# Output row built on eight neighbouring partitions of 128 columns with zero-padded weights, stored as eight rows, with filler matmuls between the last weight pieces

## Chip, cores, metric

One core of a Trainium2 chip. The metric is device time in microseconds (us); I quote the median of several executions. Times inside a profile are counted from the start of its span, which is shorter than the measured time (381.1 against 382.4 for the kernel before).

Names in the profile: PE is the matmul engine and PEld its weight loads; DVE is the vector engine, which makes the cast; POOL fills buffers at the start; SPq is the sequencer that issues the loads and the store; SBUF is the on-chip memory. The granted clock is the share of the full matmul clock that PE was allowed: below, warm is 1.00 and cold is 0.50.

## Reference

One decode token: an attention block over a cache of 65,536 keys with 4 key/value heads and 32 query heads, mixed by a scalar gate with a small gated MLP. What matters here is the end of it.

```python
q = (x @ wq)                                  # 1 x 4096, 32 heads of 128
o = softmax(q k^T * Dh**-0.5) v               # k, v: 4 heads x 65536 x 128, bf16
a = o.reshape(1, 1, 4096) @ wo                # wo: 4096 x 1024   <- the tail of the kernel
b = gmlp(x)                                   # 1 x 1024
return g * a + (1 - g) * b                    # 1 x 1024, bf16
```

The inputs are 162 MB, read once.

## The kernel before

One long stream of loads (keys, values and weights) runs on one queue through a ring of buffers. The `wo` matrix is the last 8 MB: pieces 0, 1 and 2 of 2 MB, then piece 3 in cuts of 5, 2 and 1 row blocks. A row block is 128 rows of `wo` by 1024 columns. A store of zeros stands ahead of the last load in the queue; the real store comes at the end.

```python
# constants:  QW = DO // 4   (256 columns), ovec: one column of 128 per row block, 32 of them
osrc = bass.AP(tensor=arena, offset=OFF["OROW"], ap=[[32 * NA, 4], [1, QW]])   # rows 0, 32, 64, 96

def store():
    P("SP", lambda e: e.dma_start(out[0, 0].rearrange("(q n) -> q n", n=QW), osrc), ...)

# ... the gated MLP's share (four partial rows) is summed into fb first, by float32 matmuls with
# start=True ("e4" picks the partitions 0, 32, 64, 96), long before the tail ...

out_first(3)            # softmax denominators of the last head
out_rest(3)             # normalise, select, fill ovec for the last 8 row blocks

for i, c0, c1 in [(0, 0, 8), (1, 0, 8), (2, 0, 8)] + [(3, c0, c1) for c0, c1 in WO_CUT]:
    sl, keys = use(("wo", i, c0))
    def f(e, i=i, sl=sl, c0=c0, c1=c1):
        for c in range(c0, c1):
            for q in range(4):                                  # four column groups of the array
                o = DO * (c - c0) + QW * q
                ins = e.matmul(fb[32*q:32*q+1, 0:QW], ovec[:, 8*i+c:8*i+c+1], sl[:, o:o+QW],
                               start=False, stop=(i == 3 and c == 7), tile_position=(0, 32*q), ...)
        return ins
    P("PE", f, r=[("ovec", i)] + keys, w=["fb"])
    # ... (the buffer is given back to the ring)
P("DVE", lambda e: e.tensor_copy(orow[0:97, :], fb[0:97, 0:QW]), w=["orow", "fb"])   # the cast
store()
```

Of the kernel before, what the change touches and what calls it, by code (L numbers as in the profile page):

```python
# [9 lines left out]
ALU = mybir.AluOpType  # L10
AXX = mybir.AxisListType.X
# [120 lines left out]
def bass_gated_mix__gqa_block_cached__mixer_gmlp__decode_kernel(  # L132
# [14 lines left out]
    G, Sk, Dh = A_k_cache.shape[1:]  # L147
# [4 lines left out]
    DO = A_wo.shape[1]  # L152
# [3 lines left out]
    FC = FH // 128  # L156
    OC = HQ * Dh // 128
# [3 lines left out]
    total = G * NP  # L161
# [3 lines left out]
    QP = 152  # L165
    NKT = 2
    NSC = 4
    QW = DO // 4
    FB4 = FH // 4
    SCALE = 1.0 / math.sqrt(Dh)  # L170
    GELU_C = 0.044715
# [4 lines left out]
    OFF = {}  # L176
    cur = 0

    def region(name, nbf):
        nonlocal cur  # L180
        OFF[name] = cur
        cur += (nbf + 15) // 16 * 16

    for name, n in [
        ("RING", NSUB * SUB), ("KT", NKT * 4096), ("SC", NSC * 2048), ("PSB", 2 * 1024), ("PTSB", 2 * 1024),
        ("QPAD", 4 * QP), ("IDB", 128), ("BM", 256), ("SEL", 16 * 32),
        ("M16", 32), ("MQ", 32), ("XT", KC), ("WB", 2), ("WBB", 4), ("ONEB", 128),
        ("MAXC", 2 * total), ("LP", 2 * total), ("COLS", 2 * 64), ("DM", 64), ("ONES", 256), ("QALL", 128), ("OV", OC), ("MHALF", 4),
        ("YB", FC), ("OROW", QW),
    ]:  # L190
        region(name, n)
    NA = (cur + 63) // 64 * 64
    arena = nc.alloc_sbuf_tensor("arena", [128, NA], BF16)

    def ab(name, n, o=0):
        return arena[:, OFF[name] + o:OFF[name] + o + n]

    def af(name, n, o=0):
        return arena[:, OFF[name] + 2 * o:OFF[name] + 2 * (o + n)].bitcast(F32)

    def vw(base, off, dims, p0=0, np_=128):
        ps = base.ap[0][0]
        return bass.AP(tensor=base.tensor, offset=base.offset + off + p0 * ps,
                       ap=[[ps, np_]] + [list(d) for d in dims])

    idb, bm, ones = ab("IDB", 128), af("BM", 128), af("ONES", 128)
# [2 lines left out]
    qpad, qall = ab("QPAD", 4 * QP), ab("QALL", 128)  # L209
    maxc, lp, colt = af("MAXC", total), af("LP", total), af("COLS", 64)  # L210
    mhalf = af("MHALF", 2)
    yb, ovec, orow = ab("YB", FC), ab("OV", OC), ab("OROW", QW)
    dm = af("DM", 32)
    psb, psb2 = ab("PSB", 1024), ab("PSB", 2048)
    osc, ot = ab("PSB", 512), af("PSB", 128, 256)
    col = lambda i: colt[:, i:i + 1]
    (C_GS, C_GE, C_G1, C_G, C_OMG, C_MU, C_V, C_S0, C_R0, C_S1, C_R1, C_AL, C_BE, C_T) = range(14)
    C_E4, C_G4 = 14, 16

    def gcol(g, i):  # L220
        return col(C_G4 + 12 * g + i)
# [11 lines left out]
    scp = nc.alloc_psum_tensor("scp", [128, 2048], F32)  # L233
# [4 lines left out]
    ob, mb, fb = obt[:, :], mbt[:, :], fbt[:, :]  # L238
    tb = scp[:, 1024:1536]
    tbh = tb.bitcast(BF16)  # L240
    KSC = lambda n: ("scp", n % 2)
# [3 lines left out]
    P = R.op  # L245
# [12 lines left out]
    m32 = af("SC", 32, 136)  # L258
# [4 lines left out]
    P("POOL", lambda e: e.tensor_copy(idb, idf), r=["idf"], w=["idb"])  # L263
    P("POOL", lambda e: e.memset(qpad, 0.0), w=["qpad"])
    P("POOL", lambda e: e.memset(orow, 0.0), w=["orow"])
    P("POOL", lambda e: e.memset(ones, 1.0), w=["ones"])
    P("POOL", lambda e: e.memset(oneb, 1.0), w=["oneb"])
    P("DVE", lambda e: e.memset(mb, 0.0), w=["mb"])
# [76 lines left out]
    WO_CUT = [(0, 5), (5, 7), (7, 8)]  # L345
# [2 lines left out]
    for c0, c1 in WO_CUT:  # L348
        load([("wo", 3, c0)], rows(A_wo, 3, 8)[:, DO * c0:DO * c1], WO_AT[3] + DO * c0)

    osrc = bass.AP(tensor=arena, offset=OFF["OROW"], ap=[[32 * NA, 4], [1, QW]])

    def store():
        P("SP", lambda e: e.dma_start(out[0, 0].rearrange("(q n) -> q n", n=QW), osrc), r=["orow"],
          w=["out"], dma="out")
# [5 lines left out]
    def grains(off, w):  # L361
        return list(range(off // GRAN, (off + w + GRAN - 1) // GRAN))

    def issue():

        while issued[0] < len(stream):
            n = issued[0]
            keys, off, src = stream[n]
            w = src.shape[1]
            gr = grains(off, w)  # L370
            if any(k not in used for x in gr if x in owner for k in owner[x]):
                return
            for j, x in enumerate(gr):
                owner[x] = (keys[j * len(keys) // len(gr)],)
            if n == len(stream) - 1:
                store()
            P("SP", lambda e, o=OFF["RING"] + off, w=w, src=src: e.dma_start(arena[:, o:o + w], src),  # L377
              w=[("slot", x) for x in gr], dma="s%d" % gr[0])
            issued[0] += 1

    def use(key):
        n, off, w = place[key]
        assert n < issued[0], key
        return arena[:, OFF["RING"] + off:OFF["RING"] + off + w], [("slot", x) for x in grains(off, w)]

    def done(key):
        used.add(key)
        issue()
# [7 lines left out]
    P("POOL", lambda e: e.tensor_copy(vw(bm, 0, [[8, 16], [1, 8]]), vw(m8, 0, [[0, 16], [1, 8]])), r=["m8"], w=["bm"])  # L396

    P("DVE", lambda e: e.tensor_reduce(m32, vw(idf, 0, [[1, 32], [32, 4]]), AXX, ALU.add), r=["idf"], w=["m32"])
    P("POOL", lambda e: e.tensor_copy(col(C_E4), m32[:, 0:1]), r=["m32"], w=["e4"])
    P("POOL", lambda e: e.tensor_copy(vw(sel, 0, [[16, 32], [1, 16]]), vw(m32, 0, [[1, 32], [0, 16]])),  # L400
      r=["m32"], w=["sel"])
    P("DVE", lambda e: e.tensor_reduce(mq, vw(idf, 0, [[1, 16], [16, 8]]), AXX, ALU.add), r=["idf"], w=["mq"])
    P("DVE", lambda e: e.tensor_reduce(mhalf, vw(idf, 0, [[32, 2], [64, 2], [1, 32]]), mybir.AxisListType.XY, ALU.add),
      r=["idf"], w=["mhalf"])
# [4 lines left out]
    for fe in range(4):  # L409
        P("POOL", lambda e, fe=fe: e.tensor_copy(vw(sele, 128 * fe, [[32, 4], [1, 32]]),  # L410
                                                vw(idb, 64 * (fe // 2) + fe % 2, [[0, 4], [2, 32]])),
          r=["idb"], w=[KSE])
# [5 lines left out]
    def f(e):  # L418
        for c in range(KC):
            ins = e.matmul(tb[:, c:c + 1], vw(xm, c, [[8, 128]], 0, 8), oneb[0:8, 0:1], start=(c == 0),  # L420
                           stop=(c == KC - 1), skip_group_check=True)
        return ins
# [3 lines left out]
      r=["oneb", "wsp", "bsp"], w=["mb"])  # L426
# [6 lines left out]
      r=["ones", "gs"], w=[KTB])  # L433
# [4 lines left out]
      r=["g"], w=["omg"])  # L438
# [3 lines left out]
    wqs, keys = use(("wq", 0))  # L442
# [105 lines left out]
    def out_first(g):  # L548
        def f(e):
            for h in range(2):  # L550
                ins = e.matmul(mb[:, 0:1], bm, lp[:, 2 * g + h:2 * g + h + 1], start=(h == 0), stop=(h == 1))  # L551
            return ins
        P("PE", f, r=["bm", ("lp", 2 * g), ("lp", 2 * g + 1)], w=["mb"])
# [19 lines left out]
    def out_fourth(g):  # L573
        P("DVE", lambda e: e.tensor_tensor(vw(ot, 0, [[8, 16], [1, 8]]), vw(mb, 0, [[8, 16], [1, 8]]),
                                           vw(mq, 0, [[1, 16], [0, 8]]), ALU.mult), r=["mq"], w=["psb", "mb"])

        def red(e):
            with nc.allow_low_precision(reason="one term is not zero"):
                return e.tensor_reduce(ovec[:, 8 * g:8 * (g + 1)], vw(ot, 0, [[1, 8], [8, 16]]), AXX, ALU.add)
        P("DVE", red, r=["psb"], w=[("ovec", g)])  # L580


# [24 lines left out]
    def mixer_rest(zw, zc, KZR, KZT):  # L607
# [27 lines left out]
        P("DVE", lambda e: e.scalar_tensor_tensor(yb, z2[:, 0:FC], col(C_OMG), h1, op0=ALU.mult, op1=ALU.mult),  # L635
          r=["z2", "omg", "zg"], w=["yb", KZR])

    def wout_piece():
        sl, keys = use(("wout", 0))

        def f(e):
            for c in range(FC):
                j = c % 4
                for s in range(2):
                    o = DO * c + 512 * s
                    ins = mm(e, s > 0, ob[32 * j:32 * j + 1, 512 * s:512 * (s + 1)], yb[:, c:c + 1], sl[:, o:o + 512],
                             start=(c < 4), stop=(c >= FC - 4), tile_position=(0, 32 * j), skip_group_check=True)
            return ins
        P("PE", f, r=["yb"] + keys, w=["ob"])
        done(("wout", 0))  # L650
        part = ab("KT", 2048, 4096).bitcast(F32)
        P("ACT", lambda e: e.activation(part[0:97, :], ob[0:97, :], ACTF.Copy), w=[("kt", 1), "ob"])

        def f(e):
            for q in range(4):
                ins = e.matmul(fb[32 * q:32 * q + 1, 0:QW], col(C_E4)[0:97, :], part[0:97, QW * q:QW * (q + 1)],
                               start=True, stop=False, tile_position=(0, 32 * q), skip_group_check=True)
            return ins
        P("PE", f, r=["e4", ("kt", 1)], w=["fb"])


    def k_step(n):

        for p in range(4):
            k_piece(n, p)
# [5 lines left out]
    def out_rest(g):  # L671
        out_second(g)
        out_third(g)
        out_fourth(g)
# [28 lines left out]
    for n in (12, 13, 14, 15):  # L703
        pv_piece(n)
        if n < 14:
            pt_half(n + 2)
    out_first(3)
    out_rest(3)


    for i, c0, c1 in [(0, 0, 8), (1, 0, 8), (2, 0, 8)] + [(3, c0, c1) for c0, c1 in WO_CUT]:
        sl, keys = use(("wo", i, c0))

        def f(e, i=i, sl=sl, c0=c0, c1=c1):
            for c in range(c0, c1):
                for q in range(4):
                    o = DO * (c - c0) + QW * q
                    ins = e.matmul(fb[32 * q:32 * q + 1, 0:QW], ovec[:, 8 * i + c:8 * i + c + 1],  # L718
                                   sl[:, o:o + QW], start=False, stop=(i == 3 and c == 7),
                                   tile_position=(0, 32 * q), skip_group_check=True)  # L720
            return ins
        P("PE", f, r=[("ovec", i)] + keys, w=["fb"])
        done(("wo", i, c0))
    P("DVE", lambda e: e.tensor_copy(orow[0:97, :], fb[0:97, 0:QW]), w=["orow", "fb"])  # L724
    store()

    R.ahead = 2
# [29 lines left out]
```

## Time and profile before

| | kernel before |
|---|---|
| time | 382.43 us (three executions, 382.40 to 382.46) |
| span of the profile | 381.1 us |
| bytes read | 162.01 MB, 425 GB/s over the span |
| PE instructions in the profile | 2176 (1383 matmuls, 793 weight loads) |

The chain that ended last, kernel before, from 370 us on: start, duration, what. One reads it as: the `wo` loads (345.52 + 31.08) are waited for until 376.60, then PE works through the cuts, then the cast.

```profile
345.52 31.08 DMA arena<-in_A_wo_dram
...
376.74 1.73 PE fbt L718 x28
...
378.50 0.41 PE fbt L718 x4
...
379.00 0.42 DVE arena L724
```

The same tail in the timeline: start, duration, engine, line, operation, count, and in brackets how long the engine sat idle and what ended it. The first weight load of each cut starts when that cut has landed, so the rows at 377.87 and 378.50 date the last two landings.

```profile
373.55 1.36 PE L718 MATMUL fbt<-arena 128*1 128x256 bf16 x32 [2.22 <-DMA arena<-in_A_wo_dram]
...
376.74 2.14 PE L718 MATMUL fbt<-arena 128*1 128x256 bf16 x32 [1.83 <-DMA arena<-in_A_wo_dram]
377.87 0.10 PEld L718 LDWEIGHTS fbt<-arena 128*1 128x1 bf16 x8 [0.40 <-DMA arena<-in_A_wo_dram]
378.50 0.09 PEld L718 LDWEIGHTS fbt<-arena 128*1 128x1 bf16 x4 [0.52 <-DMA arena<-in_A_wo_dram]
379.00 0.42 DVE L724 CAST arena<-fbt 97x256 bf16<-97x256 f32 x1 [9.98 <-PE fbt L718]
379.45 0.54 SPq L354 DMA_DIRECT2D out_dram<-arena  x1
```

The windows view of the kernel before: after the stretch come PE, weight loads, DVE, ACT and POOL (busy us and instructions), then the granted clock, the DMA share and GB/s. The clock is low during the last pieces.

```profile
373.50:376.70 3.20, 1.36 (x32) 0.72 (x32) 0.00 (x0) 0.00 (x0) 0.00 (x0) 0.60 0.89 363
376.70:378.90 2.20, 2.12 (x32) 0.73 (x32) 0.00 (x0) 0.00 (x0) 0.00 (x0) 0.50 0.22 87
```

The queue's own waits, kernel before: the store takes 1.1 us more after its issue.

```profile
SPq L121 <- DMA out_dram<-arena: 1.1, 1, 1.1
```

### The profile page before, as it was taken

The page shows a single profiled execution, that of the slowest core. Times are in us where ns is not written, and L with a number is a line of the kernel's source. Part 1 is how long each engine was busy: PE and PEld are TensorE (multiplying, and loading weights), DVE is VectorE, ACT ScalarE, POOL GpSimd, SP SyncE. Part 2 cuts the span into 40 slices and gives each one's busy share as a digit, 9 for nine tenths or more (in the row PEclk, how much of TensorE's full clock was granted, in tenths as well). Part 3 has the DMA queues.
Part 4 walks back from the last instruction along what each step waited for, and adds up shares of the span by engine and source line. Part 5 has one row for each costly group of instructions (what it writes and reads, how often), then busy time and mean ns, then how long its engine had stood idle before and what let it go on. Part 6 is the DMA issues. An engine that isn't in the chain of part 4 may idle for free.

```text
span 381.1 us, 2468 instructions
## 1 busy us (share of the span) xinstructions
PE 229.2 (60%) x1383; PEld 55.5 (15%) x793; DVE 204.5 (54%) x162; ACT 22.2 (6%) x23; POOL 7.5 (2%) x35
## 2 busy tenths in 40 slices
PE   0050487566558924893887238952995984549373
PEld 0010011111111200121111001220121111212031
DVE  3111596778489525956882249745875871402020
ACT  1000000010420000002000000022000000220000
POOL 4000000000000000000000000000000000000000
PEclk9997599698959975999798858985998896959776
DMA  9999999999999999999999999999999999999995
GB/s 440 434 433 413 426 387 437 440 492 420 428 433 392 426 442 440 433 420 433 454 428 440 440 440 440 421 433 440 392 420 439 457 433 426 426 408 433 423 430 223
DMA packets 4237, 162.15 MB, mean 426 GB/s; under 512 B 508, under 2 KB 516, under 8 KB 772
## 3 DMA queue, kind: packets, MB, share of 16 engines
q1 hardware_dynamic: 4192, 162.01, 98.7%
q8 instruction: 8, 0.13, 0.1%
q10 hardware_dynamic: 36, 0.00, 0.0%
q14 instruction: 1, 0.01, 0.0%
HBM read 162.01 MB, written 0.00 MB: 425 GB/s over the span
## 4 chain that ended last, share of the span: by engine, by line
DMA 63%; DVE 18%; PE 17%; issue 1%; ACTq 0%; SPq 0%; DVEq 0%
DMA arena<-in_A_k_cache_dram 41%; DVE arena L490 15%; DMA arena<-in_A_v_cache_dram 10%; DMA arena<-in_A_wo_dram 8%; PE scp L250 5%; DMA arena<-in_B_b_sp_dram 5%; PE scp L252 5%; PE obt L250 3%; PE obt L252 3%; DVE arena L527 1%; PE fbt L718 1%; ACTq L276 0%; DVE arena L563 0%; DVE arena L561 0%; SPq L377 0%
## 5 line engine op out<-in xcount | busy, mean ns | idle before, releaser
L490 DVE STREAM_TRANSPOSE arena<-arena 128x2048 f32<-128x2048 f32 x64 | 142.8, 2283 | 45.9 <-DMA arena<-in_A_k_cache_dram 31.3
L250 PE MATMUL scp<-arena 128*128 128x512 bf16 x256 | 108.9, 425 | 84.9 <-DVE arena L490 84.9
L252 PE MATMUL scp<-arena 128*128 128x512 bf16 x256 | 107.7, 421 | 0.0
L250 PE MATMUL obt<-arena 128*64 128x512 bf16 (+2 forms) x334 | 62.8, 416 | 21.3 <-DMA arena<-in_A_v_cache_dram 21.3
L252 PE MATMUL obt<-arena 128*64 128x512 bf16 (+2 forms) x334 | 61.9, 410 | 0.0
L250 PEld LDWEIGHTS scp<-arena 128*128 128x128 bf16 x256 | 26.9, 105 | 194.4 <-issue 99.5
L527 DVE STREAM_TRANSPOSE arena<-arena 128x2048 bf16<-128x2048 bf16 x7 | 16.2, 2311 | 31.3 <-PE obt L252 29.1
L250 PEld LDWEIGHTS obt<-arena 128*64 128x64 bf16 (+1 forms) x334 | 18.3, 113 | 74.5 <-issue 56.9
L522 ACT ACTIVATE arena<-arena 128x2048 bf16<-128x2048 f32 x8 | 16.0, 2003 | 218.1 <-DVE arena L519 195.0
L507 DVE TENSOR_SCALAR_CACHE_REDUCE arena<-scp 128x2048 f32<-128x2048 f32 x8 | 18.3, 2292 | 16.0 <-PE scp L252 16.0
L568 PE MATMUL mbt<-arena 128*128 128x128 bf16 x16 | 2.2, 286 | 13.6 <-DVE arena L563 13.6
L530 DVE STREAM_TRANSPOSE arena<-arena 128x1024 bf16<-128x1024 bf16 x2 | 2.5, 1245 | 12.7 <-PE obt L252 12.7
L718 PE MATMUL fbt<-arena 128*1 128x256 bf16 x128 | 6.6, 370 | 4.1 <-DMA arena<-in_A_wo_dram 4.0
L556 DVE RECIPROCAL arena<-mbt 128x1 f32<-128x1 f32 x4 | 0.6, 140 | 15.7 <-PE mbt L551 15.7
L478 POOL COPY arena<-arena 32x32 bf16<-32x32 bf16 x16 | 3.3, 204 | 236.3 <-PE scp L252 210.9
L519 DVE TENSOR_REDUCE arena<-mbt 128x1 f32<-128x32 f32 x4 | 0.8, 192 | 13.3 <-PE mbt L516 13.3
L420 PE MATMUL scp<-arena 8*128 8x1 bf16 x8 | 0.6, 197 | 10.8 <-DVE arena L415 10.8
L425 PE MATMUL mbt<-arena 1*128 1x2 bf16 x1 | 0.2, 158 | 10.4 <-DMA arena<-in_B_b_sp_dram 10.4
L724 DVE CAST arena<-fbt 97x256 bf16<-97x256 f32 x1 | 0.4, 425 | 10.0 <-PE fbt L718 10.0
L427 DVE COPY arena<-mbt 128x2 f32<-128x2 f32 x1 | 0.2, 159 | 10.4 <-PE mbt L425 10.4
L718 PEld LDWEIGHTS fbt<-arena 128*1 128x1 bf16 x128 | 3.3, 103 | 7.2 <-DMA arena<-in_A_wo_dram 3.4
L415 DVE TENSOR_TENSOR arena<-arena 8x1024 bf16<-8x1024 bf16 x1 | 1.2, 1211 | 4.9 <-DMA arena<-in_A_x_dram 4.9
(88 smaller groups left out, 48.9 us busy)
## 6 DMA issues: line engine op xcount, KB each, us to landing
arena<-in_A_k_cache_dram SPq DMA_DIRECT2D x6, 4096.0 KB, 33.2
arena<-in_A_v_cache_dram SPq DMA_DIRECT2D x2, 4096.0 KB, 26.9
arena<-in_B_w_in_dram SPq DMA_DIRECT2D x1, 7168.0 KB, 31.0
arena<-in_A_wo_dram SPq DMA_DIRECT2D x3, 2048.0 KB, 34.4
arena<-in_B_w_out_dram SPq DMA_DIRECT2D x1, 3584.0 KB, 21.8
arena<-in_A_wo_dram SPq DMA_DIRECT2D x1, 1280.0 KB, 31.1
arena<-in_A_wo_dram SPq DMA_DIRECT2D x1, 512.0 KB, 31.8
arena<-in_A_wo_dram SPq DMA_DIRECT2D x1, 256.0 KB, 31.3
```

The costliest lines, as they stand in the source:

```text
L250: return e.matmul(*a, **kw)
L252: one = e.matmul(*a, **kw).ins
L415: P("DVE", lambda e: e.tensor_tensor(vw(xm, 0, [[128, 8], [1, 128]], 0, 8), vw(xrow, 0, [[0, 8], [1, 128]], 0, 8), vw(idb, 0, [[1, 8], [0, ...
L478: P("POOL", lambda e, pb=pb: e.tensor_copy(vw(qpad, 24 + 32 * pb, [[QP, 4], [1, 8]], 32 * pb, 32), vw(qall, 8 * g, [[32, 4], [1, 8]], 32 * ...
L490: P("DVE", lambda e: e.transpose(ktb(i).bitcast(F32), sl[:, 4096 * p:4096 * (p + 1)].bitcast(F32)), r=keys[4 * p:4 * p + 4], w=[("kt", i % ...
L507: P("DVE", lambda e: e.tensor_scalar(scs(j), scp[:, :], 0.0, None, op0=ALU.add, op1=ALU.max, accum_out=maxc[:, j:j + 1]), w=[("sc", j % 2) ...
L519: P("DVE", lambda e: e.tensor_reduce(gcol(g, K_NB), mb[:, 0:32], AXX, ALU.min), w=[("nb", g), "mb"])
L522: P("ACT", lambda e: e.activation(psb2, scs(j), ACTF.Exp, bias=gcol(j // 2, K_NB), scale=SCALE, accum_out=lp[:, j:j + 1]), r=[("sc", j % 2 ...
L527: P("DVE", lambda e: e.transpose(ptsb2, psb2), r=["psb"], w=[("ptsb", 0), ("ptsb", 1)])
L530: P("DVE", lambda e: e.transpose(ptsb(n), ab("PSB", 1024, 1024 * (n % 2))), r=["psb"], w=[("ptsb", n % 2)])
L568: ins = e.matmul(mb[:, 0:128], sel[:, 128 * c:128 * (c + 1)], osc[:, 128 * c:128 * (c + 1)], start=(c == 0), stop=(c == 3))
L718: ins = e.matmul(fb[32 * q:32 * q + 1, 0:QW], ovec[:, 8 * i + c:8 * i + c + 1], sl[:, o:o + QW], start=False, stop=(i == 3 and c == 7), ti ...
```

## The change

The intent, as the diff shows it: a shorter cast (128 columns instead of 256), a store whose rows are neighbours, and a PE whose clock stays up. In the kernel before, each matmul writes one row, on the first partition of its column group (0, 32, 64, 96), so the rows lie 32 partitions apart. To bring them onto neighbouring partitions, each weight column is stored inside a block of zeros, and a window of 32 columns, shifted so that the one real column falls on the wanted partition, is the weight operand. The other 31 partitions receive zeros added. Rows 28 to 31 come from column group 0, rows 32 to 35 from group 1. The price is 8 matmuls and 8 weight loads a row block, not 4 and 4.

```diff
-    QW = DO // 4
+    NW = 8
+    QW = DO // NW
+    W0 = 32 - NW // 2
...  ovec -> ovz (zeros between the columns), e4 -> e4z (padded too), two memsets on POOL
-    osrc = bass.AP(tensor=arena, offset=OFF["OROW"], ap=[[32 * NA, 4], [1, QW]])
+    osrc = orow[W0:W0 + NW, :]
...
+    SLOTS = []
+    for h in range(NW // 2):
+        SLOTS += [(h, 0, W0 + h), (NW // 2 + h, 1, h)]
...
+    def spin(n):
+        def f(e):
+            for _ in range(n):
+                ins = e.matmul(scp[:, 0:512], idb, ab("KT", 512), start=True, stop=True)
+            return ins
+        P("PE", f, r=["idb", ("kt", 0)], w=[KSC(0)])
+
+    def wo_piece(i, c0=0, c1=8):
+        ...
+            for c in range(c0, c1):
+                for s, b, j in SLOTS:
+                    o = DO * (c - c0) + QW * s
+                    z = 31 + 32 * (8 * i + c) - j
+                    ins = e.matmul(fb[32 * b:32 * (b + 1), 0:QW], ovz[:, z:z + 32],
+                                   sl[:, o:o + QW], start=False, ..., tile_position=(0, 32 * b))
...
     out_first(3)
+    wo_piece(0)
     out_rest(3)
-    (the loop over the pieces)
-    P("DVE", lambda e: e.tensor_copy(orow[0:97, :], fb[0:97, 0:QW]), w=["orow", "fb"])
+    wo_piece(1)
+    spin(5)
+    wo_piece(2)
+    spin(3)
+    for c0, c1 in WO_CUT:
+        wo_piece(3, c0, c1)
+    P("DVE", lambda e: e.tensor_copy(orow[0:W0 + NW, :], fb[0:W0 + NW, 0:QW]), w=["orow", "fb"])
     store()
```

## The prediction

> **What bounds the kernel.** The page: 162 MB at a mean of 426 GB/s, DMA busy share 9 in 39 of 40 slices. In the chain that ended last, DMA holds 63%. The change touches no load and no reuse of the stream's buffers, so only the tail after the last loads can move. Timeline of that tail (us from the span's start): output-projection pieces 0 and 1 run together at 368.20 to 371.33, piece 2 at 373.55, the three cuts of piece 3 at 376.74, about 377.9 and 378.50; the last four matmuls take 0.41, the cast 0.42 (379.00 to 379.42), the store's issue 0.54 from 379.45, its landing about 1.1 more (waits of the DMA queue), end 381.1. At stake are these 2.6 us.
>
> **What the change does, costed.**
> 1. Cast 97x256 becomes 40x128. The 128x512 memset takes 0.485, the 128x2 copy 0.16, the 97x256 cast 0.425: about 0.16 fixed plus 1.04 ns a column. So 0.29: saves 0.13, all on the chain.
> 2. Each row block of wo takes 8 matmuls of 128 columns on two column groups, not 4 of 256 on four. In the timeline the P·V matmuls (two column groups, 512 columns) advance a pair per 0.43 us when the granted clock is 0.5 and per 0.215 when it is 1.0; the old projection fits four groups at once (a row block per 0.21 cold, 0.11 warm). So the new block needs 4x128 columns in sequence: estimate 0.43 cold, 0.215 warm.
> 3. The fillers and the earlier piece 0 are to hold the clock up. Before, the windows view shows clock 0.60 at piece 2 and 0.50 at piece 3. [...] (the pace 0.43 falls to 0.215 at 363.98, about 5 us after the PE resumed at 358.95). If warm, a block costs 0.215: what it cost before, cold. PE then ends its last cut within about -0.1 to +0.15 us of before. If cold, the cuts queue: 5, 2 and 1 blocks at 0.43 from 376.74 end near 380.35, 1.4 later than 378.91.
> 4. Fillers: 5 and 3 matmuls of 512 columns, about 1.1 and 0.65 us warm, fit the gaps of 2.2 and 1.8 us.
> 5. Store of 8x256 B instead of 4x512 B: same 2 KB[...]
> 6. Two more memsets on POOL near 3 us, hidden: the PE waits until 21.9 for a load.
>
> **Sum.** Warm (chance 70%): -0.13 on the cast, about 0 on the PE and store. Cold or partly cold: +0.4 to +1.3. Predicted 382.3 us, range 381.8 to 383.3. Faster by over 2%: 0.01; within 2%: 0.97; slower: 0.02.
>
> **What would show it.** Cast near 0.29. Granted clock 1.0 from 376.7 to the last matmul, new matmuls about 27 ns apart, the last ending 378.8 to 379.1. Store from issue to end 1.65 as before. Last load landing unchanged, near 378.45.
>
> **What would make it wrong.** A cold clock at piece 3; weight loads of 32 columns not hidden behind 128-column matmuls with two groups only (then over 27 ns apart even warm); another landing time of 256 B rows; fillers overrunning into a landed piece; a change in the stream's own rate.

The sum came to 382.3: 382.43 of the kernel before, less 0.13 for the cast, with about 0 for PE and the store. The range adds the cold clock's +0.4 to +1.3. In step 3 is what the trace showed: 0.43 us for a pair of matmuls fell to 0.215 about 5 us after PE resumed.

## More of the kernel before

The page's DMA lines of the kernel before: queue, kind, packets, MB, share of the time of 16 DMA engines. q1 carries the loads.

```profile
q1 hardware_dynamic: 4192, 162.01, 98.7%
q8 instruction: 8, 0.13, 0.1%
```

## The result, and the profile after

| | before | after |
|---|---|---|
| time, median (range) | 382.38 us (382.27 to 382.46, 6 executions) | 383.25 us (383.12 to 383.57, 6 executions) |
| ratio after / before | | 1.0024 (95% interval 1.0011 to 1.0037) |
| PE instructions in the profile | 2176 | 2464 |

Ratios are the mean time of one kernel's fast runs over that of the other's of the same rounds, so they are not quite the ratio of the medians quoted.

The change costs 0.87 us: within 2%, but a loss where I expected a gain of 0.1. The profile says where. The page's DMA lines after; there is one instruction packet more:

```profile
q1 hardware_dynamic: 4208, 162.01, 98.5%
q8 instruction: 9, 0.15, 0.2%
```

The chain that ended last, after, from 370 us on. The loads are waited for until 379.16, and PE has little to do between landings:

```profile
345.67 33.49 DMA arena<-in_A_wo_dram
...
379.20 0.62 PE fbt L685 x16
...
379.83 0.42 PE fbt L685 x8
...
380.34 0.28 DVE arena L746
```

The timeline after. Piece 2 and the first cut land 0.2 us earlier than before (373.27 and 376.40, against 373.51 and 376.60); the second and third cut land at 379.16 and 379.79, which is 1.33 and 1.34 us later. These four are landing times from the semaphore records; PE starts 0.04 to 0.14 us after them.

```profile
373.32 1.96 PE L685 MATMUL fbt<-arena 128*32 128x128 bf16 x64 [1.74 <-DMA arena<-in_A_wo_dram]
375.22 0.82 PE L674 MATMUL scp<-arena 128*128 128x512 bf16 x3
376.54 1.29 PE L685 MATMUL fbt<-arena 128*32 128x128 bf16 x40 [0.50 <-DMA arena<-in_A_wo_dram]
379.20 0.45 PEld L685 LDWEIGHTS fbt<-arena 128*32 128x32 bf16 x16 [1.54 <-DMA arena<-in_A_wo_dram]
379.83 0.23 PEld L685 LDWEIGHTS fbt<-arena 128*32 128x32 bf16 x8 [0.18 <-DMA arena<-in_A_wo_dram]
380.34 0.28 DVE L746 CAST arena<-fbt 36x128 bf16<-36x128 f32 x1 [11.78 <-PE fbt L685]
380.65 0.31 SPq L359 DMA_DIRECT2D out_dram<-arena  x1
```

The windows view after: the clock is 1.00 where it was 0.60 and 0.50.

```profile
373.50:376.70 3.20, 2.70 (x73) 2.01 (x69) 0.00 (x0) 0.00 (x0) 0.00 (x0) 1.00 0.89 364
376.70:378.90 2.20, 1.13 (x40) 0.95 (x35) 0.00 (x0) 0.00 (x0) 0.00 (x0) 1.00 0.25 88
```

The store's wait after its issue, after:

```profile
SPq L121 <- DMA out_dram<-arena: 0.9, 1, 0.9
```

The sum closes. Landings are the last of a load's sixteen completions in the trace's semaphore records.

| part of the tail | before | after | difference |
|---|---|---|---|
| last cut has landed | 378.45 | 379.79 | +1.34 |
| from there to the start of the cast (PE) | 0.55 | 0.55 | 0 |
| cast | 0.42 | 0.28 | -0.14 |
| cast's end to the store's issue | 0.03 | 0.03 | 0 |
| from the store's issue to the end | 1.64 | 1.24 | -0.40 |
| sum | | | +0.80 (span: 381.1 to 381.9; the medians differ by 0.87) |

So everything that the change meant to shorten did shorten, by 0.54 us, and the load stream took it back and more.

### What held the stream

That a DMA engine is late shows in the completions. The page counts sixteen DMA engines, and each large load has sixteen semaphore increments in the trace; I take each increment for one engine's share that has landed (the trace does not name the engine). Below, for some loads, how many us each completion came ahead of the last one (from the semaphore records; this is not a view of the page):

```
kernel before; instruction packets start at 53.1 99.9 136.3 191.8 247.3 287.2 337.4 371.8
load complete at   ahead of the last completion by
   41.21   0.52 0.48 0.47 0.45 0.43 0.42 0.41 0.39 0.35 0.33 0.32 0.27 0.25 0.22 0.06 0
   59.25   1.58 1.57 1.55 1.51 1.51 1.49 1.46 1.45 1.42 1.41 1.37 1.35 1.27 1.17 1.09 0
  319.84   1.79 1.77 1.76 1.75 1.74 1.70 1.58 1.39 1.34 0.67 0.32 0.28 0.27 0.18 0.16 0
  373.51   2.00 1.99 1.98 1.96 1.94 1.92 1.77 1.60 0.88 0.52 0.50 0.48 0.39 0.36 0.22 0
  378.45   1.92 1.89 1.87 1.84 1.83 1.70 1.55 0.82 0.51 0.49 0.46 0.44 0.37 0.34 0.18 0
kernel after; instruction packets start at 53.4 99.9 136.1 189.3 245.0 287.5 329.7 368.7 377.0
  376.40   1.74 1.73 1.72 1.70 1.68 1.60 1.53 0.84 0.21 0.20 0.19 0.18 0.17 0.16 0.05 0
  379.16   3.22 3.21 3.20 3.19 3.17 3.08 3.01 2.34 1.74 1.73 1.71 1.70 1.69 1.68 1.57 0
  379.79   3.18 3.18 3.17 3.17 3.14 3.07 3.00 2.31 1.75 1.73 1.73 1.72 1.70 1.69 1.60 0
```

Read from the top. Until 41 us all sixteen finish within 0.5 us. After the first instruction packet, one engine is about 1.1 us or more behind all the others. After every further packet one more joins the laggards, while the lead of the earliest over the last hardly grows (1.58 at 59 us, 2.00 at 373.51): by 378 in the kernel before, seven are 1.5 us or more ahead of the last, one 0.82, and the others within about 0.5. The eighth packet, at 371.8, also turned an early engine into a late one (eight values of 1.60 or more at 373.51, seven of 1.55 or more at 378.45) and delayed nothing. The lag never goes away in these runs; I take it that this is because no engine runs out of queued loads (in before_pad2074 below the queue did run dry, and the lags were gone). The one at 0.82 is not explained by the eight packets listed: it joined between 87.2 and 106.7 us, and in that stretch the trace has, beside the packet at 99.9, an instruction packet of 8192 bytes at 87.8, on another queue:

```profile
q14 instruction: 1, 0.01, 0.0%
```

Half the bytes and about half the lag fit together, but no run tests it. In the changed kernel the ninth packet came at 377.0, and after it one completion was 1.57 us behind an otherwise unchanged pattern.

The packet records of the changed kernel show, as I read them, that engine at work: from 378.1 until the store the data packets come one after the other, the first as the instruction packet ends.

```
start    end      ns    bytes
377.017  378.118  1101  16384  instruction (q8)
378.102  378.543   441   4096  wo, second cut  (159 ns each for this size just before)
378.540  378.767   227   2048  wo, third cut   (84 ns each for this size just before)
378.753  378.879   126   2048
   ... five more, 84 to 89 ns each ...
379.285  379.369    84   2048
```

I read the instruction packets on q8 as PE's program, fetched in blocks of 16,384 bytes. The spacing says so: from two microseconds ahead of the first packet to the same ahead of the eighth, PE had begun 1815 instructions in the kernel before, 259 a block. Before_pad2074 below shows the block as 256 instructions. What a block costs, the experiments show.

### The profile page after: what moved, and what is told of

It reads as the page before. It is cut to its first block, busy times and chain, and to the rows that moved or that the text cites. A ratio compares the mean times of both kernels' runs of the same rounds, so it can differ in the third digit from the quotient of the medians.

```text
span 381.9 us, 2759 instructions
## 1 busy us (share of the span) xinstructions
PE 232.8 (61%) x1527; PEld 60.5 (16%) x937; DVE 204.5 (54%) x162; ACT 22.2 (6%) x23; POOL 8.4 (2%) x37
## 4 chain that ended last, share of the span: by engine, by line
DMA 64%; DVE 17%; PE 17%; issue 1%; ACTq 0%; SPq 0%; DVEq 0%
DMA arena<-in_A_k_cache_dram 40%; DVE arena L495 15%; DMA arena<-in_A_v_cache_dram 10%; DMA arena<-in_A_wo_dram 9%; DMA arena<-in_B_b_sp_dram 5%; PE scp L253 5%; PE scp L255 5%; PE obt L253 4%; PE obt L255 3%; DVE arena L532 1%; ACTq L281 0%; SPq L382 0%; PE fbt L685 0%; DVE arena L568 0%; DVE arena L566 0%
## 5 line engine op out<-in xcount | busy, mean ns | idle before, releaser
L253 PE MATMUL obt<-arena 128*64 128x512 bf16 (+2 forms) x334 | 63.6, 426 | 21.7 <-DMA arena<-in_A_v_cache_dram 21.7
L255 PE MATMUL obt<-arena 128*64 128x512 bf16 (+2 forms) x334 | 62.8, 420 | 0.0
L685 PE MATMUL fbt<-arena 128*32 128x128 bf16 x256 | 8.2, 219 | 4.2 <-DMA arena<-in_A_wo_dram 4.2
L685 PEld LDWEIGHTS fbt<-arena 128*32 128x32 bf16 x256 | 7.2, 97 | 5.7 <-DMA arena<-in_A_wo_dram 4.7
L460 DVE CAST arena<-obt 97x1024 bf16<-97x1024 f32 x1 | 1.2, 1225 | 5.6 <-PE obt L255 5.6
```

The lines of the kernel that those rows point to most:

```text
L253: return e.matmul(*a, **kw)
L255: one = e.matmul(*a, **kw).ins
L460: P("DVE", lambda e: e.tensor_copy(psb[0:97, :], ob[0:97, :]), w=["psb", "ob"])
L685: ins = e.matmul(fb[32 * b:32 * (b + 1), 0:QW], ovz[:, z:z + 32], sl[:, o:o + QW], start=False, stop=(i == 3 and c == 7), tile_position=(0 ...
```

## The experiments

The theory: the change adds 288 PE instructions, so a ninth instruction fetch falls while `wo` is still being loaded; it holds a DMA engine for 1.1 us, and the load waits for that engine. Within it two readings: the fetch hurts because it falls late (**place**), or because it is the ninth and hits an engine already behind (**count**). The rival: something in the changed tail delays the loads, be it the eight-row store of zeros that stands in the queue, the padded weights, or the fillers' and doubled matmuls' reads of SBUF.

All twelve kernels gave the reference's result within its tolerance.

| run | time, median (range) | before, same rounds | ratio (95% interval) | fetches begun before the last cut landed |
|---|---|---|---|---|
| before_pad150 | 382.48 (382.36 to 383.65) | 382.34 | 1.0009 (0.9997 to 1.0021) | 9, the ninth at 377.8 |
| before_pad80 | 382.27 (382.17 to 382.42) | 382.34 | 0.9999 (0.9987 to 1.0011) | 9, the ninth at 377.6 |
| after_pad60 | 384.76 (382.94 to 385.68) | 382.34 | 1.0051 (1.0029 to 1.0072) | 9, the ninth at 373.0 |
| after_pad120 | 383.90 (383.20 to 385.25) | 382.34 | 1.0047 (1.0032 to 1.0062) | 10, the ninth at 372.3, one at 379.7 |
| before_pad282 | 383.69 (383.60 to 383.89) | 382.39 | 1.0035 (1.0022 to 1.0047) | 9, the ninth at 371.5 |
| after_rows4 | 381.94 (381.89 to 382.11) | 382.39 | 0.9989 (0.9976 to 1.0001) | 8 |
| after_nofill | 383.21 (383.08 to 383.57) | 382.39 | 1.0021 (1.0007 to 1.0035) | 9, the ninth at 376.8 |
| before_fill | 382.24 (382.14 to 382.32) | 382.39 | 0.9996 (0.9983 to 1.0008) | 8 |
| after_trim | 381.89 (381.63 to 382.06) | 382.33 | 0.9987 (0.9975 to 1.0000) | 8 |
| rows4_step2 | 382.36 (382.29 to 382.43) | 382.33 | 1.0000 (0.9985 to 1.0016) | 8 |
| rows4_step16 | 382.32 (382.27 to 382.36) | 382.33 | 0.9999 (0.9986 to 1.0013) | 8 |
| before_pad2074 | 407.70 (406.44 to 408.54) | 382.33 | 1.0662 (1.0645 to 1.0679) | 16 (see below) |

### Moving the fetches: before_pad150, before_pad80, after_pad60, after_pad120

The edit in all four, with 75, 40, 30 and 60 turns of the loop; it adds two PE instructions a turn, in a stretch where PE waits for a load, and moves every later fetch:

```diff
     P("DVE", lambda e: e.tensor_copy(xT, tb[:, 0:KC]), w=["xT", KTB])
+    def f(e):
+        for _ in range(75):
+            ins = e.matmul(scp[:, 0:1], idb, oneb[:, 0:1], start=True, stop=True)
+        return ins
+    P("PE", f, r=["idb", "oneb"], w=[KSC(0)])
```

> The kernel before, plus 75 one-column matmuls (150 PE instructions with their weight loads) near 11 us, while PE waits for a load. Only the place of the 16 KB instruction fetches moves: the profile of before has them each 256 PE instructions, the last at 371.8 us; counted so, this kernel's last two should come near 355 and 377 us. Fetch theory (the changed kernel is late because a fetch of 1.10 us at 377.0 held one DMA engine while it still had wo rows to bring): the last two wo cuts land about 1.3 us later, time 383.4 to 383.9. Rival (padded weights, eight-row store in the queue, or PE reads of SBUF delay the loads; none of them is in this kernel): 382.3 to 382.5, as before.

> As the other, but 40 one-column matmuls (80 PE instructions). Fetches expected near 368 and, the last one, after 379, when the data has landed. Same number of fetches as with 150. Fetch theory with the place deciding: 382.2 to 382.6. If each further fetch costs wherever it falls: about 383. Rival (nothing to do with fetches): 382.3 to 382.5 too; the pair of pads tells.

> The changed kernel plus 60 PE instructions near 11 us, nothing else. Fetches expected near 365, 373 and 378 or later, none at 377. Fetch theory: last cuts land near 378.4 again, time 381.7 to 382.1, faster than before by 0.3 to 0.7. If a fetch at 373 is not made good by then: 382.5 to 383. Rival: 383.1 to 383.5, as the changed kernel.

> The changed kernel plus 120 PE instructions near 11 us. Fetches expected near 362, 372 and 380. Fetch theory: 381.7 to 382.3 (up to 0.5 more if the fetch at 380 meets the store). Rival: 383.1 to 383.5.

Measured: on the kernel before, neither pad cost anything. The ninth fetches came at 377.8 and 377.6; by then the stream was all but over (the last data packets ended at 378.0 and 377.8), and the last two completions were 0.12 us apart in both. So my aim with 150 (counted with 256 instructions a fetch, where the mean of the kernel before was 259) was off by 0.8 us, and the pair did not test what it was meant to. One of the five executions with 150 took 383.65 with a span of 382.3, where the others had 380.9 to 381.1; a fetch that made it just in time would look like that, but that execution was not profiled.

On the changed kernel I expected a cure, and neither pad was one: the medians are above the changed kernel's 383.25, with a wide scatter (382.94 to 385.68 with 60) whose lower end meets the changed kernel's range. The traces decide: the last cut landed at 379.95 and 379.89, no earlier than the changed kernel's 379.79. That refuted the place reading: a fetch at 373.0 or 372.3 was not made good. After_pad60's completions around it:

```
after_pad60; instruction packets ... 324.8 362.5 373.0 381.9
  368.56   2.07 2.02 1.92 1.88 1.78 1.69 1.43 0.94 0.55 0.40 0.39 0.37 0.27 0.24 0.05 0
  375.15   3.76 3.71 3.60 3.57 3.46 3.37 3.11 2.62 2.23 2.08 2.08 2.06 1.96 1.93 1.74 0
  379.95   3.57 3.55 3.41 3.38 3.26 3.18 2.95 2.45 2.06 1.93 1.91 1.91 1.82 1.76 1.58 0
```

The ninth fetch again put one engine about 1.6 us behind, now from piece 2 on, which landed at 375.15 instead of 373.27. That had a second effect. The timeline and the windows of after_pad60:

```profile
375.19 3.60 PE L692 MATMUL fbt<-arena 128*32 128x128 bf16 x64 [3.43 <-DMA arena<-in_A_wo_dram]
...
380.11 2.14 PE L692 MATMUL fbt<-arena 128*32 128x128 bf16 x64
382.36 0.28 DVE L753 CAST arena<-fbt 36x128 bf16<-36x128 f32 x1 [13.79 <-PE fbt L692]
```

```profile
373.50:376.70 3.20, 1.51 (x30) 1.51 (x32) 0.00 (x0) 0.00 (x0) 0.00 (x0) 0.53 0.89 359
```

PE sat idle for 3.43 us, in the middle of which its clock fell (0.53 is the mean of the stretch), and 64 matmuls took 3.60 us instead of 1.96. From there PE, not the stream, ended last: the last landing was 379.95, but the cast began at 382.36. This is the cold case that the prediction costed at 0.43 us a row block (3.60 / 8 = 0.45). The two groups of fillers did not prevent it in the executions profiled (after_pad120's was cold too); those of about 383 us were not profiled.

### The count alone, on the kernel before: before_pad282

The same edit with 141 turns, on the kernel before.

> The kernel before plus 141 one-column matmuls (282 PE instructions) near 11 us. It has nine instruction fetches as the changed kernel has, the ninth expected near 371 us, while loads are still under way. Count theory (traces: the first eight fetches each put another DMA engine about 1.5 us behind, so the loads wait for the laggards once; the ninth hits a laggard again): from piece 2 on every wo load lands about 1.5 us later, the slowest of its sixteen completions 1.5 us behind the next; time 383.6 to 384.2, though tail code, store and cast are those of before. Rival (padding, store layout or fillers delay the loads): 382.2 to 382.6.

Measured: 383.69, 1.30 us above before in the same rounds. Its ninth fetch came at 371.5; in the kernel before an eighth came at 371.8. So the place is the same to 0.3 us, and the tail's code, cast and store are those of before. Its completions, and the end of its chain:

```
before_pad282; instruction packets 16.5 48.8 92.3 136.0 187.1 242.7 285.0 329.6 371.5
  368.36   1.75 1.74 1.67 1.58 1.57 1.54 1.38 0.71 0.33 0.29 0.26 0.23 0.07 0.02 0.01 0
  374.74   3.23 3.22 3.15 3.06 3.06 3.03 2.86 2.20 1.81 1.78 1.75 1.71 1.55 1.52 1.50 0
  379.70   3.19 3.17 3.08 3.02 3.01 3.00 2.82 2.17 1.83 1.77 1.74 1.72 1.56 1.51 1.51 0
```

```profile
345.49 32.37 DMA arena<-in_A_wo_dram
...
377.99 1.72 PE fbt L725 x23
...
379.75 0.41 PE fbt L725 x3
```

The loss of the changed kernel is reproduced with none of its tail: the last landing is 379.70 (379.79 in the changed kernel). The rival is not needed, and the count reading holds: the eighth fetch at this place costs nothing, the ninth 1.5 us on one engine.

### The changed tail without the ninth fetch: after_trim and after_rows4

After_trim leaves out work on purpose, ahead of the tail:

```diff
-            for i in range(16):
+            for i in range(2 if n in (1, 2, 5, 6, 9, 10) else 16):
                 b, t, cg = i // 8, 2 * (i % 8), i % 2
```

> The changed kernel with 28 of the 32 P·V matmuls left out in six of the sixteen key blocks (a wrong result on purpose): 252 PE instructions fewer, all of them before the tail, whose code is untouched: eight padded rows, fillers, store. PE's instruction count then crosses the ninth fetch boundary only at the program's end, so eight fetches before the data has landed. Count theory: last cut lands near 378.4, no completion 1.5 us behind the next, time 381.6 to 382.0. Rival (something in the changed tail delays the loads): 383.0 to 383.4.

Measured: 381.89, 0.44 below before, with the tail of the changed kernel untouched. Eight fetches, the eighth at 376.1, nearly where the harmful ninth had been; the last cut landed at 378.24 with the last two completions 0.09 us apart. Its chain:

```profile
376.52 1.76 PE fbt L685 x56
...
378.29 0.42 PE fbt L685 x8
...
378.80 0.28 DVE arena L746
```

After_rows4 gets there with a correct kernel, by one constant:

```diff
-    NW = 8
+    NW = 4
```

> The changed kernel with four rows of 256 columns on four neighbouring partitions (one constant). Padded weights, fillers and order stay; the projection takes 128 matmuls and as many weight loads, not 256, so PE has about 270 instructions fewer and a ninth fetch should not come before the data has landed. Count theory: last cut lands near 378.4 with no engine 1.5 us behind the rest, cast 0.42, time 381.8 to 382.2. Rival (padded weights and neighbouring rows delay the loads): 383.0 to 383.4.

Measured: 381.94, the fastest correct kernel. It is 0.45 below before and 1.3 below the changed kernel; its range (381.89 to 382.11) does not meet that of before in the same rounds (382.20 to 382.60), though the interval of the ratio just reaches 1.0001. The loads land as before (378.43, eight fetches), the cast is back to 0.42, and the store is as quick as with eight rows:

```profile
376.70 2.17 PE L685 MATMUL fbt<-arena 128*32 128x256 bf16 x32 [0.51 <-DMA arena<-in_A_wo_dram]
378.47 0.12 PEld L685 LDWEIGHTS fbt<-arena 128*32 128x32 bf16 x4 [0.30 <-DMA arena<-in_A_wo_dram]
378.98 0.42 DVE L746 CAST arena<-fbt 34x256 bf16<-34x256 f32 x1 [9.70 <-PE fbt L685]
379.43 0.28 SPq L359 DMA_DIRECT2D out_dram<-arena  x1
```

These two also clear padded weights, neighbouring rows and fillers of delaying the loads.

### What the fillers do: after_nofill and before_fill

After_nofill drops the two `spin` calls from the changed kernel. Before_fill adds `spin(5)`, `spin(3)` and the earlier piece 0 to the kernel before and leaves its matmuls, cast and store.

> The changed kernel without its eight filler matmuls. Still nine fetches, the ninth near 377, so the late landing stays. If the fillers are what holds the clock: granted clock falls near 0.5 to 0.7 at pieces 2 and 3, blocks take 0.43 us, time 383.5 to 384.5. If the fillers cause the late landing: 381.7 to 382.2.

> The kernel before with only the earlier piece 0 and the eight fillers; unpadded weights, four column groups, cast and store of before. Eight fetches. Clock 1.0 at the last cuts, the last four matmuls end 0.1 to 0.15 us sooner after the last landing; time 382.2 to 382.4 (the PE tail was 0.41 us, of which the clock can save about a third). If fillers delay the loads: about 383.

Measured: without fillers the changed kernel takes 383.21, against 383.25 with them (not the same rounds), so the medians show no gain from them; my expectation that the clock would fall at piece 2 missed. The windows view of after_nofill has 1.00 from 373.5 to 378.5 and 0.67 in the stretch after it:

```profile
376.70:378.50 1.80, 1.16 (x40) 0.98 (x36) 0.00 (x0) 0.00 (x0) 0.00 (x0) 1.00 0.32 110
378.50:380.00 1.50, 0.86 (x18) 0.86 (x20) 0.00 (x0) 0.00 (x0) 0.00 (x0) 0.67 0.03 11
```

The clock stayed up through the first cut, with PE busy for 1.97 us of the 3.20 from 373.5 and for 1.16 of the 1.80 after them, but the clock records put a fall to 0.50 at 379.02, just before the last two cuts, and from the last landing to the cast PE took 0.99 us (379.73 to 380.72) instead of 0.55. That execution was the longest of the five (383.57, the others 383.08 to 383.32). So in some executions the fillers may be worth some 0.4 us; one profile does not tell in how many. In the kernel before, with fillers and the earlier piece 0, the clock was 1.00 from 373.5 to 378.5 (0.60 from 373.5 and 0.50 from 376.7 without them), and PE needed 0.44 us from the last landing to the cast instead of 0.55. The time of 382.24 is 0.15 below before, of a size with the scatter of before. Neither moved the landings: the last is at 379.73 with nine fetches and at 378.45 with eight.

### Why the store got quicker: rows4_step2 and rows4_step16

Both take the version with four rows and put them 2, or 16, partitions apart (source pattern of the store, and the partitions that the windows aim at).

```diff
-    NW = 8
+    NW = 4
...
-    W0 = 32 - NW // 2
+    ST = 2                                   # or 16
+    W0 = 32 - ST * (NW // 2)
...
-    osrc = orow[W0:W0 + NW, :]
+    osrc = bass.AP(tensor=arena, offset=OFF["OROW"] + W0 * NA, ap=[[ST * NA, NW], [1, QW]])
... (the partitions in SLOTS, and the cast's range, follow the step)
```

> Four rows of 256 columns as in the version with four neighbouring rows, but the rows lie on every second partition (28, 30, 32, 34). The store of before (rows 32 partitions apart) took 0.54 us to issue and 1.65 from issue to end, that of four neighbouring rows 0.28 and 1.17. If a step other than one costs it: issue near 0.54 here, time near 382.3. If it is the distance of the rows: issue near 0.28, time near 381.9.

> The same with rows 16 partitions apart (0, 16, 32, 48). Step as the cause: issue 0.54, time near 382.3. Distance as the cause: issue between 0.28 and 0.54 or at 0.54. If both this and step 2 are near 0.28, neither is the cause.

Measured: 382.36 and 382.32, so 0.4 above four neighbouring rows. The store's issue took 0.62 and 0.54 us, and 1.1 us more to land in both. The line of rows4_step2, to compare with the 0.28 of after_rows4 above:

```profile
379.34 0.62 SPq L360 DMA_DIRECT2D out_dram<-arena  x1
```

A partition step of 2, 16 or 32 (the kernel before) cost this store about 0.4 us against a step of one (0.3 in its issue, 0.2 after it, rounded), and the distance did not matter: two apart was no better than sixteen or 32. Four rows of 512 bytes and eight of 256 both land in 0.9 us when they are neighbours. Why the step costs this is not shown.

### A test that broke: before_pad2074

The edit of before_pad282, and a second loop of 896 turns where PE waits for the first keys.

> The kernel before with 2074 further PE instructions: the 282 of the nine-fetch version near 11 us, and seven times 256 more as one-column matmuls near 31 us, while PE waits for the first keys. So sixteen fetches, the last at the same place in the tail (near 371 us). Rotation-of-eight theory (fetches go in turn to eight DMA engines; each round of eight costs the stream about 1.5 us once, with its first fetch): two rounds, as with nine fetches, time 383.5 to 384.0, and at the end about eight completions close together and the rest about 3 us ahead. If every fetch after the eighth cost 1.5 us: about 394. If the tail place alone cost it: 383.7, but without a lag of 3 us from early on.

Measured: 407.70, and nothing about the rotation follows. The padding ran past its gap, as PE paused after every 128 matmuls; I read the pauses as waits for its own program:

```profile
38.06 3.58 PE L481 MATMUL scp<-arena 128*128 128x1 bf16 x128 [2.45 <-issue]
45.08 3.57 PE L481 MATMUL scp<-arena 128*128 128x1 bf16 x128 [3.44 <-issue]
51.27 3.58 PE L481 MATMUL scp<-arena 128*128 128x1 bf16 x128 [2.62 <-issue]
```

The first keys were then used late, the queue of loads ran dry, and the lags were wiped out (at 92.75 all sixteen completions lay within 0.38 us). So it does not tell what a second round of eight fetches costs. Before that, its completions again show one laggard a fetch: two within 0.12 us of the last at 42.52, after two fetches, and five within 0.18 at 59.51, after five. It also shows two things: the blocks are 256 instructions (128 matmuls with their weight loads between pauses), and, on that reading, a fetch beside a full load stream left PE waiting 2.5 to 3.4 us where nothing slowed PE down in between (five of the six pauses; the last, as the stream ran dry, took 1.53).

## Why the prediction was right or wrong

The time measured, 383.25, lies in the range of 381.8 to 383.3, close to its upper edge. The point, 382.3, had the wrong sign: -0.1 was expected, +0.87 came. That it fell in the range was luck: the range's upper part stood for a cold clock, and the clock in the profiled execution was warm.

- **The cast** (step 1): 0.29 expected, 0.28 measured. It covers 36 partitions, not the 40 that I wrote.
- **The padded matmuls and the clock** (steps 2 and 3): right. Clock 1.00 at the last pieces, a row block in (1.29 - 0.22) / 5 = 0.21 us, with one matmul's mean duration of 0.22 taken off as the end of the pipeline (the matmuls overlap: piece 2's start 28 ns apart on the mean); landing to cast 0.55 before and after. Weight loads of 32 columns stayed hidden: at piece 2, 64 of them were busy for 1.79 us beside 64 matmuls in 1.96. Where the clock fell: in after_pad60 at 373.68, when PE had been idle for 1.9 us, and in the kernel before at 374.15, 0.6 us after a gap of 2.22 us had ended. What makes it fall is not shown further.
- **The fillers** (steps 3 and 4): they did no harm, as said. That they are what holds the clock in the changed kernel is not shown: without them it held to 379.02 in the one profile of after_nofill, and the medians agree (383.21 and 383.25).
- **The store** (step 5): missed. About 0 stood in the sum; -0.40 was measured. The cause is the step between the rows' partitions, shown by the two step runs. A cost of smaller rows does not show in this store: 0.9 us to land with 256-byte and with 512-byte rows.
- **The memsets** (step 6): POOL is busy 8.4 us where it was 7.5 before, and neither chain that ended last has POOL in it. The rest of step 6's thought, that what is added early is hidden, left out the program's own size.
- **The step that failed**: "The change touches no load and no reuse of the stream's buffers, so only the tail after the last loads can move", and with it "Last load landing unchanged, near 378.45". It landed at 379.79. The change touches no load, but its instructions are themselves loaded (nine packets on q8, not eight), and the completions put those packets on the engines that carry the loads. The ninth block of PE's program was fetched while `wo` was still arriving, and one engine fell 1.57 us behind the rest. Before_pad282 shows the loss without the change's tail, after_trim and after_rows4 show the changed tail without the loss.

In the prediction's own terms the sum should have read: cast -0.14, PE 0, store -0.40, last landing +1.34, so +0.80 between the two profiles.

What stays open: that the first eight fetches go to eight different DMA engines and the ninth returns to one of them is read off the completions (each of the first eight adds a laggard, the ninth a lag on top, in five kernels: the changed one, after_pad60, after_pad120, after_nofill and before_pad282). The trace does not name the DMA engine of a packet, and the test with two rounds broke. One fetch costs an engine about 1.5 us, when its packet lasts 1.1, because the next data packets are slow too (441 ns for 159, 227 and 126 for 84): 1.10 + 0.28 + 0.14 + 0.04 makes 1.57 of the 1.60 us by which the last cut's last completion trails in the changed kernel. Why they are slow stays open.

## What to carry to other kernels

In this kernel, bound by its load stream, the program's own instructions were part of that stream. In one like it, count the instruction packets in the profile's DMA lines before and after a change that adds PE instructions, and look for one load whose last completion stands alone. The same layout with half the instructions (four rows of 256 columns) kept the quick store and the clock and beat both kernels, at 381.94. For a small store at the end, put the source rows on neighbouring partitions: that was worth 0.4 us here, three times the shorter cast.
